# Memory attention, tanh-shrink and maxout on one core: token tiles of 320, 512, 320 over two batches, undivided runs of small matmuls, conversions begun earlier, one softmax for both parities

## The chip, the cores and the metric

The kernel runs on one core of a Trainium2 chip. The time is the device time of one execution in microseconds (us); the figure for a kernel is the median of its runs. One execution was recorded by the hardware profiler, and all profile rows are from it. Engines: PE multiplies matrices (PEld is its weight load), DVE, ACT and POOL work elementwise, SP issues most DMAs.

## The reference

Eight batches of 576 tokens, 8 heads of 64, 32 memory slots per head:

```python
a   = softmax(phi, axis=seq)                       # [8, 8, 576, 32]
k_m = einsum('bhsm,bhsd->bhmd', a, k); v_m = einsum('bhsm,bhsd->bhmd', a, v)
x   = softmax(q @ k_m^T / 8) @ v_m                 # -> [4608, 512]
h   = x @ w_in                                     # [512, 2048]
x   = (h - tanh(h)) @ w_out                        # [2048, 512]
m   = max(x @ w1, x @ w2, x @ w3)                  # three of [512, 768]
out = m @ w_out2                                   # [768, 512]
```

The weight matrices arrive as 64-bit floats, the rest as 32-bit floats.

## The kernel before

**Arithmetic.** A large product is made of three matmuls (`mm3`): each operand is split into a rounded part and a rest, and high x high, high x rest and rest x high are added in PSUM. `conv` turns a 64-bit weight block into such a pair: one DMA, an absolute value on ACT, five DVE instructions (lines 107, 108, 110, 112, 113), then POOL and ACT. One block of 128 x 512 (or 128 x 384) is called a conversion here.

**Stages.** The attention weights are never multiplied with `v_m` alone: `vw_gen` multiplies each head's `v_m` with its rows of `w_in` (the tile `vw`, by 8 small matmuls of 64 x 32 weights), and h = attention weights x `vw`, with a contraction of 256. The 2048 hidden features are worked in two phases of 1024. In phase 0 the attention of each batch is made (`kv_gen`, then `q_gen`: scores `sc` by 8 small matmuls, a softmax for parity e = 0 and one for e = 1, the result in `at`, also stored to DRAM), and partial results x go to DRAM; in phase 1 `at` is loaded again and the partial results are added. The last stage (lines 583 to 623) does the three-way maximum and the output.

**Steps.** A step is one tile of 288 tokens times one slice of 128 hidden features. Its work is 6 matmuls `ps_h` (`emit_h`), the chain tanh on ACT, subtraction on DVE, rounding on ACT, rest on POOL (`emit_g`, lines 399 to 403, the tile `gh`), and 12 matmuls `ps_x` (`emit_x`). Phase 0 and phase 1 have 128 steps each. In phase 0 the first two batches go twice over the tokens, four slices each time. `ps_x` has four PSUM banks, `ps_h` two, and the small matmuls share two banks under one tag `m`.

**Order.** Two queues of generators are advanced between matmul groups by `slot`: `fg` for the attention of coming batches and `vw`, `bg` for conversions; each entry has a step before which it doesn't start (a gate), and `rate` says how many advances a slot makes (in quarters). `need` runs an entry to its end. A list scheduler then places the emitted instructions, so that the order on an engine isn't that of the code. Conversions of the last stage's weights (`wb_conv`, `wz_conv`, stored to DRAM as `wb_d`, `wz_d`) and of `w_out`'s second half enter `bg` after the attention's pool is closed, at step 116.

Of the kernel before, what the change touches and what calls it, by code (L numbers as in the profile page):

```python
# [7 lines left out]
F32 = mybir.dt.float32  # L8
# [14 lines left out]
def kernel(  # L23
# [28 lines left out]
    C = 5  # L52
# [8 lines left out]
    LG = 2  # L61
    FC = 8
# [12 lines left out]
    ones = const.tile([P, P], F32, name="ones")  # L75
# [8 lines left out]
    ap = pool("attn", stack=attn)  # L84
    ps_x = pool("ps_x", PSUM, main)
# [42 lines left out]
    def wi_conv(fq):  # L128
        t = wi_p.tile([P, HP, FQ], F32, tag="wi", bufs=3, name="wi")
# [36 lines left out]
    def phi_gen(b):  # L166
# [6 lines left out]
        pm = ps_m.tile([P, 2, 2, P], F32, tag="m", bufs=2, name="ps_mx")  # L173
# [9 lines left out]
        V.tensor_tensor(out=ph, in0=ph, in1=pm[:, 1].rearrange("p i (h m) -> p (i h) m", m=M)[:, :, None, :].to_broadcast([P, H, C, M]), op=ALU.subtract)  # L183
# [10 lines left out]
    def kv_mm(b):  # L194
        ph = ph_t.pop(b)
        ps = ps_m.tile([P, 2, 256], F32, tag="m", bufs=2, name="ps_kv")
# [22 lines left out]
        pt = ps_m.tile([P, 2, P], F32, tag="m", bufs=2, name="ps_t")  # L219
# [15 lines left out]
    def q_gen(b, hfs):  # L235
# [7 lines left out]
        for hf in hfs:  # L243
            qT = []
            for g in range(2):
                t = ap.tile([P, 2, NH], F32, tag="qT", bufs=3, name="qT")
# [5 lines left out]
            scs = [ps_m.tile([P, NH], F32, tag="m", bufs=2, name="sc") for e in range(2)]  # L252
            for r in range(HP):
                for e in range(2):
                    pp = slice(64 * e, 64 * e + 64)
                    T.matmul(scs[e][32 * r:32 * r + 32], kT[b][pp, r], qT[r // 2][pp, r % 2], start=True, stop=True)
            yield
            o = slice(hf * NH, (hf + 1) * NH)
            for e in range(2):
                s = ap.tile([P, JH, M], F32, tag="s", bufs=2, name="s")  # L260
                V.transpose(out=s.rearrange("p j m -> p (j m)"), in_=scs[e])
                st = ap.tile([P, JH, 3], F32, tag="st", bufs=2, name="st")
                V.reduce_max(st[:, :, 0], s, axis=AX.X)
                V.tensor_tensor(out=s, in0=s, in1=st[:, :, 0:1].to_broadcast([P, JH, M]), op=ALU.subtract)
                yield
                S.activation(s, s, AF.Exp, scale=0.125)
                yield
                V.reduce_sum(st[:, :, 1], s, axis=AX.X)
                V.tensor_scalar(st[:, :, 2], st[:, :, 1], 1e-9, None, ALU.add)
                V.reciprocal(st[:, :, 2], st[:, :, 2])  # L270
                yield
                G.tensor_tensor(out=s, in0=s, in1=st[:, :, 2:3].to_broadcast([P, JH, M]), op=ALU.mult)
                yield
                aT = ap.tile([P, NH], F32, tag="aT", bufs=2, name="aT")
# [11 lines left out]
    def vw_gen(ph, b, fq):  # L286
        while 2 * ph + fq not in wi:
            bg.need("wi")
        t = at_p.tile([P, 2, 2, FQ], F32R, tag="vw", bufs=4, name="vw")
        pss = [ps_m.tile([P, FQ], F32, tag="m", bufs=2, name="ps_w") for e in range(2)]  # L290
        for r in range(HP):
            for e in range(2):
                pp = slice(64 * e, 64 * e + 64)
# [363 lines left out]
```

## Time and profile before

| | us |
|---|---|
| median of 3 runs (1485.02 to 1493.65) | 1491.73 |
| profiled execution, own time | 1483.24 |
| its span, first to last instruction | 1481.5 |
| PE busy | 1401.1 (95%) |
| DVE busy | 657.2 (44%) |
| POOL busy | 475.3 (32%) |
| ACT busy | 443.9 (30%) |

Busy times are averages over stages that differ. Steps 0 to 16 end at about 156 us, step 112 begins at 463, phase 1 (step 128) at 522, the last stage at 881. Matmul records overlap, so what a matmul costs is read from start to start, not from its duration. A weight tile read as 64-bit halves or plain 32-bit floats gives two matmul records for an instruction.

### The profile page before, as it was taken

What the parts mean: (1) busy time and instruction counts of PE and PEld (TensorE: products, weight loads), DVE (VectorE), ACT (ScalarE), POOL (GpSimd) and SP (SyncE); (2) the same over time, 40 slices, a digit from 0 to 9 for tenths busy, and PEclk for the clock granted to TensorE, in tenths of its full rate; (3) what the DMA queues carried; (4) which work ended last, traced back from release to release, by engine and by line L of the source; (5) the groups of instructions that cost most, each with busy time, mean ns of one, the idle gap of its engine ahead of it and who ended that gap; (6) DMA issues with size and microseconds to landing.
All of it is one profiled execution on the core that took longest, in us unless ns stands there. A gap on an engine that the chain in (4) does not pass through costs nothing.

```text
span 1481.5 us, 23564 instructions
## 1 busy us (share of the span) xinstructions
PE 1401.1 (95%) x9344; PEld 1167.8 (79%) x9344; DVE 657.2 (44%) x1225; ACT 443.9 (30%) x975; POOL 475.3 (32%) x508
## 2 busy tenths in 40 slices
PE   2587999999999999999999999999999999999998
PEld 1264887988897778788899998888888888888887
DVE  3789945546557988677433231211212111111110
ACT  1244443445344444444433331111111111111110
POOL 0356434334436756465533322111111111111110
PEclk9986999999999999999999999999999999999999
DMA  7765736445514358876422135110101010100001
GB/s 182 169 197 156 211 116 161 113 117 141 144 55 165 108 178 252 278 215 206 159 97 65 62 129 206 36 36 29 44 15 43 17 48 15 45 20 15 15 15 43
DMA packets 199150, 159.87 MB, mean 108 GB/s; under 512 B 96128, under 2 KB 182144, under 8 KB 197248
## 3 DMA queue, kind: packets, MB, share of 16 engines
q1 hardware_dynamic: 197312, 145.79, 34.0%
q0 software_dynamic: 1728, 12.58, 2.4%
q8 instruction: 73, 1.20, 0.3%
q14 instruction: 37, 0.30, 0.1%
HBM read 105.64 MB, written 52.69 MB: 107 GB/s over the span
## 4 chain that ended last, share of the span: by engine, by line
PE 77%; DVE 10%; DMA 5%; SPq 4%; issue 2%; ACT 2%; POOL 1%; DVEq 0%; POOLq 0%; ACTq 0%
PE ps_w L95 10%; PE ps_w L94 10%; PE ps_w L93 10%; PE ps_x L93 7%; PE ps_x L94 7%; PE ps_x L95 7%; PE ps_h L93 4%; PE ps_h L94 3%; PE ps_h L95 3%; PE ps_o L94 3%; PE ps_o L93 3%; PE ps_o L95 3%; PE ps_w L294 3%; SPq L161 2%; DVE cvb L110 2%
## 5 line engine op out<-in xcount | busy, mean ns | idle before, releaser
L403 POOL TENSOR_TENSOR gh<-th,gh 128x288 fp32r<-128x288 f32 x256 | 217.2, 851 | 312.6 <-ACT gh L402 257.3
L94 PE MATMUL ps_x<-gh,wo 128*128 128x288 f32 x1024 | 300.5, 302 | 1.9 <-POOL gh L403 1.9
L95 PE MATMUL ps_x<-gh,wo 128*128 128x288 f32 x1024 | 294.8, 297 | 0.0
L93 PE MATMUL ps_x<-gh,wo 128*128 128x288 f32 x1024 | 264.2, 303 | 1.8 <-DVE xo L443 1.0
L95 PE MATMUL ps_w<-xh,wb 128*128 128x512 f32 x648 | 254.9, 393 | 0.0
L94 PE MATMUL ps_w<-xh,wb 128*128 128x512 f32 x648 | 254.4, 393 | 0.0
L93 PE MATMUL ps_w<-xh,wb 128*128 128x512 f32 x648 | 253.8, 392 | 0.0
L597 POOL TENSOR_TENSOR mh<-m,mh 128x512 fp32r<-128x512 f32 x54 | 71.1, 1318 | 489.0 <-ACT mh L596 489.0
L94 PEld LDWEIGHTS ps_x<-gh,wo 128*128 128x128 f32 x1024 | 195.2, 191 | 26.5 <-issue 16.0
L93 PEld LDWEIGHTS ps_x<-gh,wo 128*128 128x128 f32 x1024 | 180.1, 192 | 24.7 <-issue 14.2
L400 DVE TENSOR_TENSOR th<-ps_h,th 128x288 f32<-128x288 f32 x256 | 114.4, 449 | 184.8 <-ACT th L399 184.4
L95 PEld LDWEIGHTS ps_x<-gh,wo 128*128 128x128 f32 x1024 | 194.8, 191 | 0.7 <-issue 0.5
L93 PE MATMUL ps_h<-at,vw 128*128 128x288 f32 x512 | 160.0, 313 | 27.6 <-DVE th L400 15.8
L593 DVE TENSOR_TENSOR m<-ps_w,m 128x512 f32<-128x512 f32 x54 | 37.3, 692 | 305.6 <-PE ps_w L95 305.6
L399 ACT ACTIVATE th<-ps_h 128x288 f32<-128x288 f32 x256 | 105.0, 410 | 177.7 <-PE ps_h L95 169.1
L402 ACT CAST gh<-th 128x288 fp32r<-128x288 f32 x256 | 110.0, 432 | 157.2 <-DVE th L400 145.7
L94 PE MATMUL ps_h<-at,vw 128*128 128x288 f32 x512 | 155.5, 304 | 1.6 <-POOL at L278 1.5
L95 PE MATMUL ps_h<-at,vw 128*128 128x288 f32 x512 | 154.7, 303 | 0.0
L93 PEld LDWEIGHTS ps_h<-at,vw 128*128 128x128 f32 x512 | 98.4, 193 | 57.7 <-DVE th L400 24.4
L94 PEld LDWEIGHTS ps_w<-xh,wb 128*128 128x128 f32 x648 | 121.7, 188 | 27.9
L93 PEld LDWEIGHTS ps_w<-xh,wb 128*128 128x128 f32 x648 | 121.7, 188 | 27.5
L95 PEld LDWEIGHTS ps_w<-xh,wb 128*128 128x128 f32 x648 | 121.7, 188 | 27.2
(81 smaller groups left out, 1783.6 us busy)
## 6 DMA issues: line engine op xcount, KB each, us to landing
xd<-xo SPq DMA_DIRECT2D x36, 576.0 KB, 3.8
raw<-in_moe_w_out_dram SPq DMA_DIRECT2D x22, 512.0 KB, 4.3
qt<-in_q_dram SPq DMA_DIRECT2D x128, 72.0 KB, 3.1
at_d<-at SPq DMA_DIRECT2D x16, 576.0 KB, 3.8
at<-at_d SPq DMA_DIRECT2D x8, 1152.0 KB, 5.9
raw<-in_moe_w_dram SPq DMA_DIRECT2D x24, 384.0 KB, 3.6
wb_d<-cs SPq DMA_DIRECT2D x72, 128.0 KB, 3.4
xo<-xd SPq DMA_DIRECT2D x16, 576.0 KB, 4.2
```

The lines of the kernel that those rows point to most:

```text
L93: T.matmul(o, w[0], x[0], start=start, stop=False)
L94: T.matmul(o, w[0], x[1], start=False, stop=False)
L95: T.matmul(o, w[1], x[0], start=False, stop=stop)
L110: V.scalar_tensor_tensor(out=b, in0=hw, scalar=0xC0000000, in1=b, op0=ALU.bitwise_and, op1=ALU.bitwise_or)
L161: DMA.dma_start(out=t[64 * e + 32 * h:64 * e + 32 * h + 32, r], in_=src[e, h, r])
L294: T.matmul(pss[e][32 * r:32 * r + 32], vT[b][pp, r], wi[2 * ph + fq][pp, r], start=True, stop=True)
L399: S.activation(th, ps, AF.Tanh)
L400: V.tensor_sub(th, ps, th)
L402: S.copy(gh[:, 0], th)
L403: G.tensor_sub(gh[:, 1], th, f(gh[:, 0]))
L593: V.tensor_max(m, pss[1], m)
L597: G.tensor_sub(mh[:, 1], m, f(mh[:, 0]))
```

## The change

**Tiles.** The two batches that phase 0 begins with keep tiles of 288. All other tokens go in pairs of batches: 1152 tokens as tiles of 320, 512 and 320. The tile of 512 holds 256 tokens of either batch, so its `ps_h` is made of two groups of 6 matmuls with 256 columns each. Phase 0 has 104 steps, phase 1 96. Partial results lie in one DRAM tensor `xd[0]`; the second pass over the first two batches loads and adds the first, so that phase 1 adds one block and no second one (`xb` goes).

**Small matmuls.** The two banks get tags of their own, `m0` and `m1`. `small` makes the first of a group's 8 matmuls also wait until DVE has released bank 1, and ties the 8 in their order.

**Softmax.** Both parities lie in one tile of 18 x 32, so one maximum, subtraction, exponential, sum and so on does what two did; the two transposes out of PSUM stay.

**Conversions.** The last stage's weights enter `bg` at step 32 instead of step 116. `wi_conv(2)` moves from a gate at step 36 to the point where the attention's pool is closed (step 90), ahead of `w_out`'s second half. Gates and rates change: `kv_gen` still 20 steps before a batch's first step, `q_gen` 16, `vw` 8 and 6, each also held until a buffer is free; rates fall from 10 and 8 to 6 and 2 at step 32, `bg` back to 8 at step 90.

**Last stage.** The input x is loaded in four pieces through two buffers instead of in one.

```diff
+    def bank(i, shape, name):
+        return ps_m.tile(shape, F32, tag=f"m{i}", bufs=1, name=name)
+    def small(mms):
+        ins = [T.matmul(o, w, x, start=True, stop=True).ins for o, w, x in mms]
+        if freed[1] is not None:
+            tc.add_manual_dep(ins[0], freed[1].name, ...Sync..., reason="both banks")
+        for a, b in zip(ins, ins[1:]):
+            tc.add_manual_dep(b, a.name, ...NoSync..., reason="side by side")
...
-            scs = [ps_m.tile([P, NH], F32, tag="m", bufs=2, name="sc") for e in range(2)]
+            scs = [bank(e, [P, NH], "sc") for e in range(2)]
+            small([(scs[e][32 * r:32 * r + 32], kT[b][...], qT[r // 2][...]) for r in range(HP) for e in range(2)])
...
-            for e in range(2):
-                s = ap.tile([P, JH, M], F32, tag="s", bufs=2, name="s")
+            s = ap.tile([P, J2, M], F32, tag="s", bufs=1, name="s")
+            for e in range(2):
+                freed[e] = V.transpose(out=s[:, e * JH:(e + 1) * JH]..., in_=scs[e]).ins
...
-            V.tensor_sub(t[:, e, 1], pss[e], f(t[:, e, 0]))
+            freed[e] = V.tensor_sub(t[:, e, 1], pss[e], f(t[:, e, 0])).ins
...
+                tiles[ph] += [pieces(t0, 320), pieces(t0 + 320, 512), pieces(t0 + 832, 320)]
...
+        for b, s0, n in pcs:
...
+            for kc in range(2):
+                mm3(ps[:, c0:c0 + n], (w[:, kc, 0, f0:f0 + P], w[:, kc, 1, f0:f0 + P]), (at[:, 0, kc, o], at[:, 1, kc, o]), kc == 0, kc == 1)
...
+        add = ph or t0 < NXI and fc >= 4
+        if fc == 4 and add or final and not add:
+            emit_x.xo = ga_p.tile([P, KD, NT], F32, tag="xo", bufs=1, name="xo")[:, :, :nt]
+            if add:
+                DMA.dma_start(out=emit_x.xo, in_=xd[0][:, :, o])
...
-    bg.add("wi", wi_conv(2), 36)
...
+            aq = max([s0 - AHEAD + 4] + [last_u[bb - 3, fq] - LG for fq in range(2) if bb > 2])
...
+    for g in last_w:
+        bg.add("last", g, start[0, 2])
+    rate[:] = 6, 2
...
+    bg.add("wi2", wi_conv(2))
     bg.add("wo1", chain(*[wo_conv(fc, wo1) for fc in range(8, 16)]))
```

On PE, in phase 0, this is the place of one `vw` group of batch 3 (`vT_92`; line 294 before) among the `ps_x` matmuls of one step.

```order
L93 MATMUL ps_x_2492<-gh,wo_1107 128x288
L294 MATMUL ps_w<-wi,vT_92 32x512 x2
L94 MATMUL ps_x_2490<-gh,wo_1107 128x288
L95 MATMUL ps_x_2490<-gh,wo_1107 128x288
L94 MATMUL ps_x_2491<-gh,wo_1107 128x288
L95 MATMUL ps_x_2491<-gh,wo_1107 128x288
L94 MATMUL ps_x_2492<-gh,wo_1107 128x288
L95 MATMUL ps_x_2492<-gh,wo_1107 128x288
L294 MATMUL ps_w<-wi,vT_92 32x512 x6
L93 MATMUL ps_x_2493<-gh,wo_1107 128x288
```

The same group in the changed kernel (the small matmuls are line 106 now):

```order
L94 MATMUL ps_x_2134<-gh,wo_944 128x320
L94 MATMUL ps_x_2135<-gh,wo_944 128x320
L106 MATMUL ps_w<-wi,vT_92 32x512 x8
L95 MATMUL ps_x_2132<-gh,wo_944 128x320
L96 MATMUL ps_x_2132<-gh,wo_944 128x320
```

The 8 matmuls stood in two pieces around six others and now stand together. Over the whole order `vw` stands in 74 such runs before and 45 now, for 32 groups, and the scores `sc` in 20 and 16, for 16 groups.

On DVE, at the start of the stretch with most conversions (step 113 before), `cva` and `cvb` are the conversions' tiles and `th` is the subtraction that PE's next steps need:

```order
L113 SCALAR_TENSOR_TENSOR cva<-raw,cva 128x512
L443 COPY xo<-ps_x_5151 128x288
L400 TENSOR_TENSOR th<-ps_h,th 128x288
L443 COPY xo<-ps_x_5153 128x288
L107 TENSOR_SCALAR cva<-cva 128x512
L108 TENSOR_SCALAR cvb<-cva 128x512
L110 SCALAR_TENSOR_TENSOR cvb<-raw,cvb 128x512
L107 TENSOR_SCALAR cva<-cva 128x512
L112 TENSOR_SCALAR cva<-cvb 128x512
L400 TENSOR_TENSOR th<-ps_h,th 128x288
```

In the changed kernel, at steps 88 to 90, the corresponding stretch reads:

```order
L434 TENSOR_TENSOR th<-ps_h,th 128x512 x2
L122 TENSOR_SCALAR cva<-cva 128x512
L123 TENSOR_SCALAR cvb<-cva 128x512
L125 SCALAR_TENSOR_TENSOR cvb<-raw,cvb 128x512
L122 TENSOR_SCALAR cva<-cva 128x512
L127 TENSOR_SCALAR cva<-cvb 128x512
L123 TENSOR_SCALAR cvb<-cva 128x512
L128 SCALAR_TENSOR_TENSOR cva<-raw,cva 128x512
L125 SCALAR_TENSOR_TENSOR cvb<-raw,cvb 128x512
L127 TENSOR_SCALAR cva<-cvb 128x512
L128 SCALAR_TENSOR_TENSOR cva<-raw,cva 128x512
L434 TENSOR_TENSOR th<-ps_h,th 128x512
```

Up to ten conversion instructions, two whole conversions, stand between two subtractions where five stood.

On SP, in the second pass over the first two batches, the store of one tile's sums (`xd`) and the load of the next tile's partial sums (`xo`) now stand like this; before, this pass had no load:

```order
L472 DMA xd_109<-xo 512x1x288
L333 DMA wb_d_97<-cs 128x2x128
L333 DMA wb_d_98<-cs 128x2x128
L333 DMA wb_d_99<-cs 128x2x128
L115 DMA raw<-in_moe_w_dram 128x768
L295 DMA at_d_1399<-at 512x1x288
L458 DMA xo<-xd_109 128x4x288
```

The load stands behind stores of a conversion's result and of an attention result, which wait for POOL.

## Rows read from the trace of the kernel before

**Rows 1.** The page: granted TensorE clock in 40 slices of 37 us, tenths of full speed.
```profile
PEclk9986999999999999999999999999999999999999
```

**Rows 2.** Stages: us, busy (count) by engine, granted clock, DMA share, GB/s.
```profile
0.00:156.20 156.20, 95.91 (x749) 63.19 (x750) 115.94 (x208) 46.07 (x97) 63.23 (x67) 0.87 0.68 174
156.20:209.40 53.20, 51.99 (x524) 43.47 (x523) 40.34 (x85) 23.96 (x58) 24.09 (x28) 1.00 0.69 195
209.40:264.00 54.60, 52.23 (x525) 44.86 (x524) 28.08 (x62) 21.13 (x52) 18.99 (x25) 0.97 0.48 120
264.00:313.00 49.00, 49.00 (x527) 43.33 (x526) 28.15 (x63) 21.34 (x52) 19.01 (x25) 1.00 0.53 134
463.00:522.00 59.00, 53.52 (x355) 42.61 (x354) 53.82 (x77) 27.06 (x61) 41.14 (x35) 1.00 0.38 132
522.00:623.00 101.00, 94.88 (x637) 78.43 (x637) 78.73 (x146) 45.31 (x108) 59.76 (x65) 0.97 0.74 235
840.50:859.50 19.00, 19.00 (x146) 19.00 (x145) 5.12 (x12) 6.65 (x16) 6.48 (x8) 1.00 0.20 63
880.80:1481.50 600.70, 595.83 (x2593) 486.56 (x2592) 107.74 (x161) 91.47 (x156) 75.27 (x62) 1.00 0.14 45
```

**Rows 3.** The tanh of line 399 in one stage: us, ACT busy (count).
```profile
840.50:859.50 19.00, 3.29 (x8) 1.00 0.20 63
```

**Rows 4.** Small matmuls of line 294 by stage: PE busy, PEld busy.
```profile
463.00:522.00 59.00, 9.47 (x46) 1.30 (x46) 1.00 0.38 132
522.00:623.00 101.00, 14.60 (x80) 1.97 (x80) 0.97 0.74 235
```

**Rows 5.** PE in order of time, last stage: start, us, what.
```profile
1000.01 0.39 PE L93 MATMUL ps_w<-xh,wb 128*128 128x512 f32 x1
...
1009.99 0.39 PE L95 MATMUL ps_w<-xh,wb 128*128 128x512 f32 x1
```

**Rows 6.** PE in order of time around a part and a whole small group.
```profile
345.47 1.06 PE L294 MATMUL ps_w<-wi,vT 64*32 64x512 f32 x8
...
784.05 0.29 PE L95 MATMUL ps_h<-at,vw 128*128 128x288 f32 x1
784.27 1.09 PE L294 MATMUL ps_w<-wi,vT 64*32 64x512 f32 x16
785.29 0.40 PE L93 MATMUL ps_h<-at,vw 128*128 128x288 f32 x1
785.53 0.29 PE L94 MATMUL ps_h<-at,vw 128*128 128x288 f32 x1
```

**Rows 7.** DVE groups by shape: busy us, mean ns, idle before.
```profile
L400 DVE TENSOR_TENSOR th<-ps_h,th 128x288 f32<-128x288 f32 x256 | 114.4, 449 | 184.8 <-ACT th L399 184.4
L299 DVE TENSOR_TENSOR vw<-ps_w,vw 128x512 fp32r<-128x512 f32 x64 | 42.4, 681 | 19.4 <-ACT vw L297 19.1
L110 DVE SCALAR_TENSOR_TENSOR cvb<-raw,cvb 128x512 uint32<-128x512 uint32 x38 | 33.7, 887 | 0.7
L113 DVE SCALAR_TENSOR_TENSOR cva<-raw,cva 128x512 f32<-128x512 uint32 x38 | 33.6, 884 | 0.7
L108 DVE TENSOR_SCALAR cvb<-cva 128x512 uint32<-128x512 uint32 x38 | 28.2, 741 | 0.7
L107 DVE TENSOR_SCALAR cva<-cva 128x512 f32<-128x512 f32 x38 | 24.9, 656 | 18.0 <-ACT cva L105 17.8
L112 DVE TENSOR_SCALAR cva<-cvb 128x512 uint32<-128x512 uint32 x38 | 23.7, 624 | 0.4
L110 DVE SCALAR_TENSOR_TENSOR cvb<-raw,cvb 128x384 uint32<-128x384 uint32 x24 | 18.1, 754 | 0.5
```

**Rows 8.** One line alone: DVE line 110, ns min/median/max.
```profile
L110 DVE SCALAR_TENSOR_TENSOR cvb<-raw,cvb x62: 541/692/1761, 30.7 to 717.8; 128x512 uint32<-128x512 uint32 x38, 128x384 uint32<-128x384 uint32 x24
```

**Rows 9.** What PE waited for after 16 us: us, times, longest.
```profile
PE ps_h L93 <- DVE th L400: 15.8, 12, 2.8
```

**Rows 10.** DMA issues: count, KB each, median us to landing.
```profile
xd<-xo SPq DMA_DIRECT2D x36, 576.0 KB, 3.8
xo<-xd SPq DMA_DIRECT2D x16, 576.0 KB, 4.2
```

More of the change, by code (lines that the diff above doesn't have):

```diff
@@ L84 @@
     ap = pool("attn", stack=attn)
+    ones = ap.tile([P, P], F32, name="ones")
     ps_x = pool("ps_x", PSUM, main)
@@ L265, in q_gen @@
[L265 to L274, printed above, removed]
@@ L287, in vw_gen @@
         while 2 * ph + fq not in wi:
-            bg.need("wi")
+            bg.need("wi2")
         t = at_p.tile([P, 2, 2, FQ], F32R, tag="vw", bufs=4, name="vw")
[L290 to L293, printed above, removed]
-                T.matmul(pss[e][32 * r:32 * r + 32], vT[b][pp, r], wi[2 * ph + fq][pp, r], start=True, stop=True)
+        pss = [bank(e, [P, FQ], "ps_w") for e in range(2)]
+        small([(pss[e][32 * r:32 * r + 32], vT[b][64 * e:64 * e + 64, r], wi[2 * ph + fq][64 * e:64 * e + 64, r])
+               for r in range(HP) for e in range(2)])
         yield
@@ L362, in slot, with pieces @@
                 tr.step(now[0])
[L365 to L374 removed]
+    def pieces(t0, n):
+        out, t = [], t0
+        while t < t0 + n:
+            b, s0 = divmod(t, NS)
+            k = min(t0 + n - t, NS - s0)
+            out.append((b, s0, k))
+            t += k
+        return t0, n, out
@@ L411, in emit_x @@
     def emit_x(i):
-        ph, b, s0, fc, first, final = steps[i]
+        ph, (t0, nt, pcs), fc, first, final = steps[i]
         while 8 * ph + fc not in wo_t:
@@ L447, in emit_x @@
         if final:
-            DMA.dma_start(out=d[:, :, s0:s0 + NH], in_=xo)
+            DMA.dma_start(out=xd[ph][:, :, o], in_=emit_x.xo)
     hooks = {}
@@ L486 @@
     bg.add("wo", chain(*[wo_conv(fc, wo_p) for fc in range(1, 4)]))
-    bg.add("wo", chain(*[wo_conv(fc, wo_p) for fc in range(4, FC)]), 10)
-    bg.add("wi", wi_conv(2), 36)
+    bg.add("wo", chain(*[wo_conv(fc, wo_p) for fc in range(4, FC)]), 6)
+    last_w = [wb_conv(w, kc, g) for g in range(2) for w in range(3) for kc in range(KD)] + [wz_conv(j) for j in range(J)]
     fg.add("kv", kv_gen(1))
@@ L517 @@
     wo1 = wo1_p.__enter__()
+    bg.q, rest = bg.q[:1], bg.q[1:]
+    bg.add("wi2", wi_conv(2))
     bg.add("wo1", chain(*[wo_conv(fc, wo1) for fc in range(8, 16)]))
-    for g in range(2):
-        for w in range(3):
-            for kc in range(KD):
-                bg.add("wb", wb_conv(w, kc, g))
-    for j in range(J):
-        bg.add("wb", wz_conv(j))
-    run(start[0, B - 1] + 4, start[1, 0] - 2)
+    bg.q += rest
+    rate[1] = 8
+    run(start[0, B - 1] + 2, start[1, 0] - 2)
     bg.need("wo1")
+    rate[1] = 2
     run(start[1, 0] - 2, start[1, 0])
```

188 lines of the change are left out of this document (99 added, 89 removed).

## The prediction

> **What bounds the kernel now.** I read the stages first [rows 2], then the order of PE inside them, then who waits. In the last stage PE is busy 595.8 of 600.7 us; its matmuls are neither fewer nor smaller after the change, so I carry it over at 600.7. Before it, three pictures alternate. From 840.5 to 859.5 nothing but steps runs: 8 tanh [rows 3] in 19.0 us, so a step of 18 matmuls of 288 columns costs 2.375 us, one matmul 132 ns. From 264 to 313 one batch's attention is added: 49.0 us for 16 steps, 38.0 of them steps and 11.0 attention on PE, with DVE busy only 28.2 us. From 463 to 623 the conversions are added: 160 us for 48 steps; DVE is busy 53.8 of 59.0 us (91%) in the first part, and PE waits for DVE's subtraction, 15.8 us in 12 places of the whole trace [rows 9]. The first 156 us are DVE's too: 115.9 us busy, PE 95.9, and the granted clock is 0.87 there, with slices at 0.8 and 0.6 [rows 1, 2], which is the 1.2 GHz level for part of them. So PE sets the end nearly everywhere after 156 us, and DVE where conversions crowd.
>
> **Runs of small matmuls.** A whole group takes 784.27 to 785.29; from the matmul ahead of it (784.05) to the second behind it (785.53) are 1.48 us instead of two gaps of 132 ns, so a run costs 1.21 us [rows 6]. A part of a group costs nearly the same: 1.06 us against 1.09 for sixteen records [rows 6]. The price is thus per run and not per matmul. By the order there are 74 runs of `vw` before and 45 after, of which 7 and 4 fall into the first 16 steps, where DVE decides; from 67 to 41 are 26 x 1.21 = 31.5 us. Two runs of `sc` fewer after step 16, priced somewhat lower since they stream 288 columns: 2. A run that must wait for both banks is placed later in the order; I price the wait at nothing, because the order puts a step's `ps_x` matmuls ahead of it. Without that cover the step's other matmuls, queued behind it on PE, and the tanh that waits for them are late: rival 3.
>
> **Matmul counts.** 512 columns take (1009.99 - 1000.01) / 44 = 226.8 ns, first and last of 45 starts [rows 5]. With 132 ns for 288 the line has 0.423 ns a column and 10.1 ns a matmul: 145.5 ns for 320, 118.4 for 256. A slice of a pair of batches needs 3 x 12 `ps_x` matmuls where four tiles of 288 need 48: 12 fewer, 96 in eight slices, 672 over the 7 pairs of both phases (3 and 4); `ps_h` keeps its count, 6 + 12 + 6 for 4 x 6. That gives 672 x 10.1 = 6.8 us. No row has 256 columns with full weights: if such a matmul took the 132 ns of 288, 672 of them would take back 9.1 us; if it took half of 226.8, 3.3 more would be gained. I take the line, as both neighbours lie on it.
>
> The Trainium skill (TensorE: Matmul & The Clock Gate, Back-to-back issue gap) gives a lone matmul N / 2.4 + 2.5 ns at full clock. By that the 672 would be worth 672 x 2.5 = 1.7 us, an estimate from the page, instead of 6.8; the trace's 226.8 ns for 512 columns lies 11 ns above that formula, and the sum goes by the rows.
>
> **Stalls that go.** 463 to 623 holds 160 us; 48 steps are 114.0, the small matmuls 9.47 + 14.60 = 24.1 us busy [rows 4], that is 22 runs at 1.09, or 26.6 us by the full price. 19.4 us are left: waits for DVE, small gaps, and a clock of 0.97. By the new order 17 of the 24 conversions of 384 columns stand before step 56, so this stretch changes its shape: I take these 19.4 out and put in the new ones below. 209 to 264 took 54.6 against 49.0 [rows 2]; with one run more there, 4 of the 5.6 are a stall of the old order, and I let them go too.
>
> **The first 156 us.** DVE bounds them. Merged softmaxes save the fixed part of six instructions on each half of a batch: four halves, some 1 us each, 4 us. The bounds are 0 (nothing, if the chain of waits and not the load decides) and 10 (the slices at the lower clock shrink too).
>
> **New load on DVE.** Here I add DVE's work between tanh subtractions, in its new order, and compare it with PE's steps. A conversion of 512 columns is 887 + 884 + 741 + 656 + 624 ns = 3.79 us [rows 7]; one of 384, scaled by 754 / 887, 3.2. A batch's attention with its `vw` and copies is 28.15 - 16 x 0.449 = 21.0 us [rows 2, 7].
> - Steps 88 to 104: 14 conversions (53.1), one of 384 begun (1.9), 8 `vw` subtractions at 0.681 (5.4), the tanh subtractions (8 at 0.48, 8 at 0.68: 9.3), half a batch's softmax and four copies (7): 77 us. PE there: 8 steps of 512 (12 x 226.8 + 12 x 118.4 ns = 4.14 us), 8 of 320 (2.62), 7 runs: 62.6 us. At the 91% that DVE reached in its fullest stretch, 77 would take 85, 22 too long; a lead of about two steps absorbs some 5. I take 18, from bounds of 5 (all of the lead, and DVE fully busy) and 33 (conversions a sixth dearer).
> - Steps 16 to 56: 17 conversions of 384 and 2 of 512 (62), three batches' attention (63), tanh subtractions (20), 16 additions of the second pass (7): 152 us, against PE with 113 us of steps and 3 x (11.0 - 1.2) of attention, 142. Same bound, 167; but the second pass leaves PE three or more steps ahead by the order. 11, from 0 to 36. This holds the second pass's reload as well: store 3.8, load 4.2 [rows 10] and two issues make more than 8 us against the 9.5 us of four steps, so its cover is thin, and SP has stores waiting for POOL in between.
> - Steps 64 and 88: the odd batch of a pair is needed 8 steps after the even one; the order shows PE's lead falling from three steps to two there. Two waits of 2 us, under the longest of 2.8 [rows 9]: 4, from 0 to 6.
> - Phase 1 until step 128, with 11 conversions left: 3, from 0 to 8.
>
> The conversions' stores `wb_d` move along. Where they stood the DMA share was 0.74, where they go it is 0.69 and 0.48 [rows 2]; I price that at nothing, and its loss of cover is in the 36 above.
>
> Phase 1 beyond that has DVE idle before and after, and dropping `xb`'s additions there gains nothing.
>
> **Sum.** -31.5 - 2 - 6.8 - 19.4 - 4 - 4 + 18 + 11 + 4 + 3 = -31.7 us. On the profiled execution's own 1483.2 that is 1451.5; on the median, which is 8.5 higher, 1460. I forecast the middle, 1456.
>
> **Rivals.**
> 1. DVE's backlog vanishes in PE's lead. For: 264 to 313 shows DVE far from full beside attention. Against: 91% in 463 to 522 already cost PE. Then 31 of the 36 us of new stalls fall away: 1425. Chance 0.20.
> 2. Slower: DVE becomes the bound of steps 16 to 56 and 88 to 104. The place is the subtraction `th` standing behind two conversions; the point is reached when a conversion beside attention and longer POOL instructions costs 4.5 us instead of 3.79. Line 110 alone ranges from 541 to 1761 ns [rows 8]. Then 162 and 87 us of DVE work at 91% are 178 and 96 against 142 and 62.6 of PE: 69 instead of 29, and with the waits at 64 and 88 no longer covered some 4 more: 1500. For: those ranges; against: the mean held over stages that were as full. Chance 0.07.
> 3. The runs become whole, but PE stands waiting for both banks. If half of the 41 runs wait the 1.3 us that a wait for DVE takes on the mean [rows 9], 27 us come back: 1483. For: the second phase still has 23 runs in parts, which shows banks being late; against: 8 of 8 together is where the order put them while other work was at hand. Chance 0.12.
>
> The Trainium skill (SBUF — State Buffer, Who interferes with whom) says that a DVE instruction in a two-port mode or with two SBUF inputs and a POOL instruction exclude each other for a whole instruction. By that, POOL instructions of 512 columns instead of 288 hold a conversion up longer, which speaks for rival 2; the spread of line 110 (541 to 1761 ns, an extra of up to 1.2 us) agrees with such blocking.
>
> **Numbers.** My own case, 1456 with 1436 to 1476, has 0.61. Less than 0.5% (about 7.5 us, what a measurement of this kernel tells from no change) counts as the same. Faster: all but 0.01 of my case, rival 1, half of rival 3, 0.86; same: the other half of it, 0.02 of rival 2 and the 0.01, 0.09; slower: the rest of rival 2, 0.05. The range takes in rival 1's price and stops short of rival 2: 1425 to 1482.
>
> **What would show it.** The last stage must again take about 601 us. Runs in the trace of phase 0 must have 16 records each, and small matmuls' busy time must fall by some 30 us. Stage times: about 152 us to step 16, 150 to 155 for steps 16 to 56, 78 to 82 for steps 88 to 104, 81 for a pair in the later phase 1 (75 of steps, five runs). DVE must be busiest (over 90%) in steps 88 to 104 and PE's waits for `th` must lie there. I am wrong if the gain comes with the old number of runs, if PE waits at the small matmuls for DVE, or if the second phase, which has DVE to spare, gains less than 25 us.

## The result and the profile after

The changed kernel took 1503.71 us (median of 7 runs, 1497.64 to 1506.05) against 1485.22 us for the kernel before on the same chip (7 runs): over all runs a ratio of 1.010, with a 95% interval of 1.0073 to 1.0128. The forecast was 1456 us, range 1425 to 1482: wrong in sign and outside the range. The profiled execution has a span of 1498.0 us and an own time of 1499.8 us, 16.5 us more than before by either.

The stages of the changed kernel, in the columns of [rows 2]: steps 0 to 16, 16 to 56, 56 to 88, 88 to 104 (the end of phase 0), 104 to 128, the rest of phase 1, the last stage:
```profile
0.00:158.20 158.20, 87.14 (x747) 62.96 (x747) 113.81 (x185) 45.48 (x91) 64.29 (x61) 0.86 0.65 171
158.20:334.80 176.60, 155.07 (x1480) 128.51 (x1479) 139.44 (x246) 72.73 (x154) 93.29 (x90) 0.96 0.78 216
334.80:472.50 137.70, 131.76 (x1370) 111.63 (x1368) 75.61 (x131) 53.58 (x109) 50.33 (x47) 1.00 0.42 115
472.50:551.50 79.00, 64.14 (x342) 48.63 (x343) 75.04 (x96) 31.84 (x61) 50.38 (x39) 0.96 0.42 137
551.50:649.80 98.30, 88.08 (x536) 72.55 (x535) 61.74 (x98) 40.91 (x85) 54.10 (x49) 0.95 0.65 215
649.80:897.30 247.50, 247.50 (x1613) 220.25 (x1614) 70.40 (x130) 82.39 (x165) 75.12 (x75) 1.00 0.23 78
897.30:1498.00 600.70, 595.88 (x2594) 486.67 (x2592) 109.08 (x161) 92.83 (x158) 74.01 (x62) 1.00 0.15 46
```
The last stage is the same to 0.1 us, so the 16.5 us lie ahead of it. To see what they are, the stretch from step 16 to the last stage in one row, first before, then after:
```profile
156.20:880.80 724.60, 709.37 (x6007) 618.11 (x6006) 433.55 (x858) 306.38 (x723) 336.78 (x380) 0.99 0.48 146
```
```profile
158.20:897.30 739.10, 686.55 (x5336) 581.57 (x5335) 422.24 (x698) 281.44 (x569) 323.23 (x298) 0.98 0.47 142
```
Length less PE's busy time is PE's idle time: 15.2 us before, 52.5 after. **PE works 22.8 us less and waits 37.3 us longer.** With 2.0 us more up to step 16 that is the 16.5. The saving of work came about, and more than all of it was given back in waits. The longest waits of PE after step 16 (what waited <- what released it: us, times, longest), first in the kernel before, then in the changed one:
```profile
PE ps_h L93 <- DVE th L400: 10.2, 10, 1.9
PE ps_w L294 <- DVE s L261: 2.0, 1, 2.0
PE ps_x L94 <- POOL gh L403: 1.9, 7, 0.6
```
```profile
PE ps_h L94 <- DVE th L434: 15.6, 17, 1.9
PE ps_x L94 <- ACT gh L436: 6.6, 1, 6.6
PE ps_w L106 <- DVE vw L312: 6.5, 5, 2.3
PE ps_x L95 <- POOL gh L437: 6.1, 12, 1.2
PE ps_w L106 <- POOL wi L131: 4.8, 1, 4.8
PE ps_mx L190 <- DVE vw L312: 4.5, 4, 1.7
```
The wait for the tanh subtraction grew from 10.2 to 15.6 us ([rows 9] has 15.8, but counts the first 156 us too). New are waits of small matmuls for the subtraction `vw`, which frees their bank (11.0 us in two lines; `ps_mx` are transposes that use bank 1 too), one wait of 4.8 us for a converted block of `w_in` (`wi`), and longer waits for `gh`. One of the waits for `vw` in full, on PE and then on DVE (start, us, what, in brackets idle before and releaser):
```profile
537.37 0.31 PE L94 MATMUL ps_h<-at,vw 128*128 128x320 f32 x1
...
539.22 0.31 PE L94 MATMUL ps_x<-gh,wo 128*128 128x320 f32 x1
...
539.95 0.31 PE L96 MATMUL ps_x<-gh,wo 128*128 128x320 f32 x1
542.61 1.04 PE L106 MATMUL ps_w<-wi,vT 64*32 64x512 f32 x2 [2.35 <-DVE vw L312]
543.58 0.42 PE L94 MATMUL ps_h<-at,vw 128*128 128x320 f32 x1
```
```profile
535.84 0.48 DVE L434 TENSOR_TENSOR th<-ps_h,th 128x320 f32<-128x320 f32 x1
536.24 1.34 DVE L122 TENSOR_SCALAR cva<-cva 128x512 f32<-128x512 f32 x1
537.61 0.98 DVE L123 TENSOR_SCALAR cvb<-cva 128x512 uint32<-128x512 uint32 x1
538.63 1.67 DVE L125 SCALAR_TENSOR_TENSOR cvb<-raw,cvb 128x512 uint32<-128x512 uint32 x1
540.33 0.43 DVE L127 TENSOR_SCALAR cva<-cvb 128x512 uint32<-128x512 uint32 x1
540.67 0.68 DVE L312 TENSOR_TENSOR vw<-ps_w,vw 128x512 fp32r<-128x512 f32 x1
541.27 0.68 DVE L128 SCALAR_TENSOR_TENSOR cva<-raw,cva 128x512 f32<-128x512 uint32 x1
541.88 0.68 DVE L312 TENSOR_TENSOR vw<-ps_w,vw 128x512 fp32r<-128x512 f32 x1
542.48 0.48 DVE L434 TENSOR_TENSOR th<-ps_h,th 128x320 f32<-128x320 f32 x1
```
The first small matmul starts when both `vw` subtractions are done; these stand behind four conversion instructions that take 4.4 us. Behind it on PE stand six `ps_h` matmuls that need neither subtraction. But they need a bank: of the two that `ps_h` has, the one freed by the subtraction at 535.84 went to the matmuls from 537.37 on, and the other is freed by the subtraction at 542.48, which stands behind the same conversion instructions and ends at 542.96. Without the small matmul ahead of them they could have started some 0.6 us earlier, no more. So two parts of the change meet here, the wait for both banks and the conversions; in this place the conversions set most of the time, and the experiments take the two apart.

### The profile page after: what moved, and what is told of

Its sections match the earlier page's. It is cut to its first block, busy times and chain, and to the rows that moved or that the text cites. A ratio compares the mean times of both kernels' runs of the same rounds, so it can differ in the third digit from the quotient of the medians.

```text
span 1498.0 us, 21579 instructions
## 1 busy us (share of the span) xinstructions
PE 1369.6 (91%) x8672; PEld 1131.2 (76%) x8672; DVE 645.1 (43%) x1043; ACT 419.8 (28%) x817; POOL 461.5 (31%) x420
## 4 chain that ended last, share of the span: by engine, by line
PE 66%; DVE 13%; DMA 8%; SPq 5%; issue 3%; POOL 3%; ACT 2%; DVEq 0%; ACTq 0%; POOLq 0%
PE ps_w L96 10%; PE ps_w L95 10%; PE ps_w L94 10%; PE ps_x L94 5%; PE ps_x L95 5%; PE ps_x L96 5%; DMA wb_d<-cs 3%; PE ps_o L95 3%; PE ps_o L94 3%; PE ps_o L96 3%; PE ps_h L94 3%; PE ps_h L96 3%; PE ps_h L95 3%; DVE cvb L125 2%; SPq L176 2%
## 5 line engine op out<-in xcount | busy, mean ns | idle before, releaser
L437 POOL TENSOR_TENSOR gh<-th,gh 128x320 fp32r<-128x320 f32 (+2 forms) x200 | 209.7, 1050 | 320.3 <-ACT gh L436 311.4
L95 PE MATMUL ps_x<-gh,wo 128*128 128x320 f32 (+2 forms) x800 | 271.0, 341 | 6.7 <-POOL gh L437 6.5
L94 PE MATMUL ps_x<-gh,wo 128*128 128x320 f32 (+2 forms) x800 | 257.0, 343 | 11.8 <-ACT gh L436 6.6
L96 PE MATMUL ps_x<-gh,wo 128*128 128x320 f32 (+2 forms) x800 | 265.6, 335 | 0.7 <-POOL wo L137 0.7
L434 DVE TENSOR_TENSOR th<-ps_h,th 128x320 f32<-128x320 f32 (+2 forms) x200 | 106.4, 534 | 197.8 <-ACT th L433 197.7
L94 PE MATMUL ps_h<-at,vw 128*128 128x320 f32 (+2 forms) x512 | 160.1, 313 | 32.5 <-DVE th L434 20.9
L94 PEld LDWEIGHTS ps_x<-gh,wo 128*128 128x128 f32 x800 | 150.8, 194 | 38.9 <-issue 17.7
L95 PEld LDWEIGHTS ps_x<-gh,wo 128*128 128x128 f32 x800 | 154.5, 193 | 27.9 <-POOL gh L437 14.5
L96 PEld LDWEIGHTS ps_x<-gh,wo 128*128 128x128 f32 x800 | 153.8, 193 | 10.9 <-issue 1.0
L625 DVE TENSOR_TENSOR m<-ps_w,m 128x512 f32<-128x512 f32 x54 | 37.3, 691 | 283.0 <-PE ps_w L96 283.0
L96 PE MATMUL ps_h<-at,vw 128*128 128x320 f32 (+2 forms) x512 | 155.5, 305 | 1.0 <-DVE vw L312 1.0
L95 PE MATMUL ps_h<-at,vw 128*128 128x320 f32 (+2 forms) x512 | 155.1, 303 | 0.0
L436 ACT CAST gh<-th 128x320 fp32r<-128x320 f32 (+2 forms) x200 | 99.7, 499 | 162.4 <-DVE th L434 150.6
L433 ACT ACTIVATE th<-ps_h 128x320 f32<-128x320 f32 (+2 forms) x200 | 94.8, 476 | 177.1 <-PE ps_h L96 168.8
```

What stands on the lines that cost most here:

```text
L433: S.activation(th, ps, AF.Tanh)
L434: V.tensor_sub(th, ps, th)
L436: S.copy(gh[:, 0], th)
L437: G.tensor_sub(gh[:, 1], th, f(gh[:, 0]))
L625: V.tensor_max(m, pss[1], m)
```

## The experiments

Theory A: the conversions beside the attention. Theory B: the fixed banks and the wait for both. Theory C: the tiles across two batches. Ratios are to the kernel before, run beside each kernel on the same chip (its median was 1483.9 to 1485.3 us in the five sets), taken over all runs, with their 95% intervals; they can differ by 0.001 from the ratio of two medians. The edits are shortened; `...` marks what is left out.

**1. Conversions after the attention again** (changed kernel, `e1_late`)
```
-    for g in last_w: bg.add("last", g, start[0, 2])
-    rate[:] = 6, 2
+    rate[:] = 6, 8
 ...
     bg.add("wo1", ...)
+    for g in last_w: bg.add("last", g)
```


> The changed kernel with one part undone: the conversions of the last stage's weights start only when the attention is finished (after step 90 of phase 0, eight pieces of work per four slots, as in the kernel before), everything else stays. Theory A (the conversions beside the attention hold up ACT, DVE and SyncE's queue, and PE waits for these): steps 16 to 104 shrink from 393 us to 355 to 370, the stretch after step 104 gives back some 5 to 15 us, time 1465 to 1485 us. Theory B (the two shared banks and the both-banks wait of the small matmuls do it): steps 16 to 104 stay at 385 to 395 us, time 1497 to 1510 us. Theory C (tiles across two batches need the odd batch 8 steps after the even one): as B.

1483.72 us, ratio 0.9989 (0.9971 to 1.0007). Theory A: the time is at the upper end of what was expected, and steps 16 to 104 took 372.5 us, just over the 370. Steps 16 to 56 of this kernel:
```profile
153.10:310.90 157.80, 146.17 (x1473) 124.91 (x1472) 86.19 (x157) 56.77 (x120) 55.67 (x56) 0.99 0.58 153
```
18.8 us less than 176.6, DVE 53 us less busy. Steps 104 to 200 took 11 us more (356.7 against 345.8), which is what the conversions cost where they stand now. The first 16 steps, ahead of the edit, were 5.1 us shorter (153.1 for 158.2); why is open.

**2. A deeper buffer for the conversions** (changed kernel, `e2_cab3`)
```
-        t = cv_p.tile([P, 2, 512], F32R, tag="cs", bufs=1, name="cs")
+        ab = cv_p.tile([P, 2, 512], U32, tag="cvab", bufs=3, name="cvab")   # in place of cva, cvb, cs
```


> The changed kernel, with the conversions where the change puts them, but without the single buffer cs: the two halves of a converted weight are written in place into a pair of work tiles that has three buffers, and stored from there. Theory A1 (ACT's rounding waits for the store that still reads cs, and tanh waits behind it): steps 16 to 104 shrink from 393 us by 15 to 30 us, and the 8.7 us wait of ACT's rounding at 559 us goes; time 1470 to 1488 us. Theory A2 (it is the number of instructions and the place of the stores in SyncE's queue, not the buffer): time within 6 us of the changed kernel's 1504 us. B and C: no change, 1497 to 1510 us.

1503.17 us, 1.0130 (1.0098 to 1.0161): A2. One place had seemed to matter most: ACT waits for the single buffer `cs`, tanh stands behind it, and PE waits 6.6 us for `gh` (the second line of the waits above):
```profile
569.35 0.51 ACT L135 CAST cs<-cva 128x384 fp32r<-128x384 f32 x1 [8.69 <-DMA wb_d<-cs]
569.76 0.43 ACT L433 ACTIVATE th<-ps_h 128x320 f32<-128x320 f32 x1
```
It was the largest single wait, and its stretch did shrink (steps 104 to 128: 91.6 us for 98.3), but the time did not: the largest wait of a trace need not be what sets the time.

**3. Tiles of 288** (changed kernel, `e3_t288`)
```
-  tiles[ph] += [pieces(t0, 320), pieces(t0 + 320, 512), pieces(t0 + 832, 320)]
+  tiles[ph] += [pieces(t0 + i * NH, NH) for i in range(4)]
```


> The changed kernel with tiles of 288 tokens of one batch throughout (four in place of 320, 512, 320), all else as changed. Theory C (the pairs of batches make the attention late): steps of 16 to 56 us lose their waits, time 1475 to 1490 us. Theories A and B: the waits stay, the number of matmuls and of tanh, subtraction and rounding instructions goes up again; a pair of batches takes 0.5 to 2 us longer in either phase, time 1500 to 1520 us.

1486.66 us, 1.0014 (0.9997 to 1.0030): by its time theory C, but not by its reason, since steps 16 to 56 did not get shorter (179.7 us for the same tokens); the gain is scattered. Experiment 11 turns its sign.

**4. No added dependences** (changed kernel, `e4_loose`)
```
-        if freed[1] is not None: tc.add_manual_dep(ins[0], freed[1].name, ..., reason="both banks")
-        for a, b in zip(ins, ins[1:]): tc.add_manual_dep(b, a.name, ..., reason="side by side")
```


> The changed kernel without the two added dependences of the small matmuls (the first no longer waits for both banks, and the eight need not stand side by side); the banks themselves stay as changed. Theory B: the waits for the subtraction of vw go from in front of the big matmuls, time 1480 to 1495 us. Theories A and C: the runs that are split again cost 1.2 us each, waits elsewhere stay; time 1500 to 1515 us.

1485.92 us, 1.0014 (0.9996 to 1.0032): theory B. Steps 16 to 56 take 178.4 us (176.6 with the dependences); steps 88 to 104 fall from 79.0 to 69.3, though DVE also has 11.4 us less to do in them (63.7 for 75.0), since work moved to the steps behind. So A and B both hold, and mostly in different places.

**5. Only the small matmuls' part** (kernel before, `f3_b_small`)
```
-        pss = [ps_m.tile([P, FQ], F32, tag="m", bufs=2, name="ps_w") for e in range(2)]
-        for r in range(HP): ...
+        pss = [bank(e, [P, FQ], "ps_w") for e in range(2)]
+        small([...])                     # likewise sc, ps_mx, ps_kv, ps_t
```

> The kernel before with one part of the change alone: two banks of one tile each for the small matmuls, and each group of eight put side by side behind the release of both banks; tiles, softmaxes and conversions as before. The prediction's step (about 26 runs fewer at 1.2 us each, nothing lost): TensorE's busy time up to the last stage falls by some 25 to 30 us and the time to 1455 to 1467 us. Theory W (the busy time falls, but TensorE then waits as much longer, since the chain from the banks' release to the next group sets the pace): time 1480 to 1490 us. Theory B (the wait for both banks costs more than the runs did): 1492 to 1505 us.

1494.92 us, 1.0081 (1.0056 to 1.0106): theory B. This row answers to the first of the two long rows in the section on the result:
```profile
160.70:889.80 729.10, 691.91 (x6007) 615.14 (x6005) 434.77 (x850) 301.81 (x721) 337.28 (x379) 0.99 0.48 144
```
PE busy 17.5 us less, idle 37.2 instead of 15.2, and the first 16 steps 4.5 us longer. The part on which the forecast counted most made the kernel before slower by itself; experiment 13 shows how much of that comes with the fixed banks alone.

**6. Only the conversions' part** (kernel before, `f4_b_spread`)
```
+    run(0, 32)
+    for g in last_w: bg.add("last", g, 32)
+    rate[1] = 2
+    run(32, start[0, B - 1] + 4)
 ...
```

> The kernel before with another part alone: the last stage's weights are converted from step 32 of phase 0 on, beside the attention, two pieces of work per four slots, instead of after it; all else as before. Theory A (the conversions beside the attention hold up what TensorE waits for): steps 16 to 64 (156.6 us before) take 170 to 180 us, steps 104 to 160 (187.3 us before) give back 5 to 20 us, time 1487 to 1500 us. The prediction's step (stalls in steps 112 to 160 go, the attention hides the conversions): 1465 to 1478 us.

1489.17 us, 1.0031 (1.0013 to 1.0050): theory A. Steps 16 to 64, 156.8 us before [rows 2, its second to fourth row], and steps 104 to 200, 303.1 us before:
```profile
155.80:331.80 176.00, 162.32 (x1586) 136.97 (x1585) 149.39 (x305) 81.96 (x200) 106.17 (x118) 0.96 0.78 210
465.10:745.30 280.20, 270.73 (x1969) 237.43 (x1969) 162.97 (x303) 119.01 (x274) 138.09 (x142) 0.99 0.45 149
```
19.2 us lost early (10 more in steps 64 to 104, 133.3 for 123.2), 22.9 given back late.

**7. Both undone** (changed kernel, edits 1 and 4, `f1_late_loose`)

> The changed kernel with two parts undone at once: conversions after the attention, and no dependences added to the small matmuls. Alone the first gave 1483.7 us and the second 1485.9 us, 20 and 18 us under the changed kernel. If the two costs lie in different places (conversions in steps 16 to 56, both banks in steps 88 to 104) they add: 1465 to 1472 us. If they are one and the same slack (either edit relaxes the one chain): 1478 to 1487 us.

1469.34 us, 0.9906 (0.9883 to 0.9929): the two costs add, and what is left of the change is worth 15 us. Its waits after step 16, complete:
```profile
PE ps_h L94 <- DVE th L430: 10.6, 15, 2.0
PE ps_x L95 <- POOL gh L433: 4.1, 5, 1.5
PE ps_x L94 <- DVE xo L461: 2.8, 2, 2.2
PE ps_mx L186 <- DVE vw L308: 2.6, 2, 1.6
PE ps_w L106 <- DVE vw L308: 1.7, 3, 0.7
```

**8. Edits 1 and 3 together** (`f2_late_288`)

> The changed kernel with conversions after the attention and tiles of 288 tokens of one batch throughout. Alone 1483.7 and 1486.7 us. If the two costs add: 1464 to 1471 us; if they are one slack: 1478 to 1487 us. The clean part of phase 1 gives the tiles' own price: 0.6 us less per pair of batches with 288 than with 320, 512, 320 (81.9 against 82.5 us in the runs so far).

1481.70 us, 0.9991 (0.9975 to 1.0008): the second case. With late conversions 288 gains nothing to speak of (1483.72 with the longer tiles).

**9. The two dependences apart** (edit 1 and one half of edit 4; `h2_sync` keeps the wait, `h1_chain` the order)
```
-        for a, b in zip(ins, ins[1:]): tc.add_manual_dep(b, a.name, ..., reason="side by side")     # h2_sync
-        if freed[1] is not None: tc.add_manual_dep(ins[0], freed[1].name, ..., reason="both banks")  # h1_chain
```

> The changed kernel with conversions after the attention, and of the two added dependences only one: the first of eight small matmuls waits until both banks are free, but the eight need not stand side by side. With both dependences 1483.7 us, with neither 1469.3 us. If the wait for both banks is the price (rival 3 of the prediction): 1480 to 1487 us. If it is the fixed order of the eight: 1467 to 1473 us.

> The changed kernel with conversions after the attention, and of the two added dependences only the other one: the eight small matmuls stand side by side, but the first does not wait for both banks. With neither dependence 1469.3 us (63 runs from step 16 to the last stage, TensorE idle for 22.3 us there), with the wait alone 1484.5 us (61 runs, 42.5 us idle). If whole groups without the wait save runs at about 1 us each and TensorE's idle time stays near 22 us: 1460 to 1468 us. If the second matmul of a group, standing in TensorE's queue behind the first, then waits for its bank and holds up all that follows: idle 35 to 45 us, 1478 to 1487 us.

The wait alone: 1484.51 us, 0.9996 (0.9982 to 1.0009). The order alone: 1478.22 us, 0.9956 (0.9933 to 0.9978). From step 16 on, with neither, with the wait, with the order:
```profile
150.90:867.10 716.20, 693.95 (x5336) 584.91 (x5335) 422.00 (x708) 281.12 (x573) 324.28 (x302) 0.99 0.49 148
```
```profile
148.60:881.70 733.10, 690.59 (x5334) 585.00 (x5324) 421.92 (x710) 280.21 (x571) 328.94 (x302) 0.98 0.48 145
```
```profile
152.00:876.10 724.10, 701.68 (x5282) 585.14 (x5275) 425.69 (x704) 280.47 (x571) 327.77 (x303) 0.99 0.48 147
```
Idle 22.3, 42.5 and 22.4 us. With the wait for both banks come the whole 20 us of idle time; it buys 3.4 us of work. The first expectation's first case holds. The order costs no waiting, but the eight did not become whole: 76 runs of small matmuls (`vw` and `sc`) in place of 63, and 7.7 us more work. That is neither case of its expectation: the idle time of the first, the time of the second. Whole groups without the wait were not had this way.

Where the idle time lies with the wait alone (three of the lines; for neither dependence see experiment 7):
```profile
PE ps_h L94 <- DVE th L432: 16.0, 11, 5.1
PE ps_w L106 <- POOL wi L129: 4.8, 1, 4.8
PE ps_w L106 <- DVE s L273: 3.8, 2, 2.2
```
Directly ahead of small matmuls stand 11.1 us, against 4.3 with neither: 7 of the 20 us. Of these, 4.8 are one wait for a converted block of `w_in`, which the changed kernel and `e1_late` have too, and `e4_loose` and `f1_late_loose`, without the wait for both banks, don't. The other 13 us lie ahead of the large matmuls, and the longest of these waits, 5.1 us at 616, comes of ACT, where tanh stands behind a rounding that waits for a load of the last stage:
```profile
614.39 0.62 ACT L576 CAST xh<-xr 128x512 fp32r<-128x512 f32 x1 [8.16 <-DMA xr<-xd]
```
So the dependence also moved other work to worse places. How much of the 20 us is waiting for the banks themselves was not separated.

**10. Conversions thin in phase 1; two softmaxes** (both on `f1_late_loose`)
```
     bg.need("wo1")
+    rate[1] = 3                                                        # h3_slow
-            s = ap.tile([P, J2, M], F32, tag="s", bufs=1, name="s")    # h4_two_softmax
+            for e in range(2):
+                s = ap.tile([P, JH, M], F32, tag="s", bufs=2, name="s")
 ...                                                                    # as before the change
```

> The changed kernel without the added dependences, and with the conversions after the attention, spread thinly over phase 1 (three pieces of work per four slots in place of eight from step 104 on). Theory A (what counts is how much DVE, ACT and POOL work stands beside TensorE's in one stretch): steps 104 to 160, 210.5 us with the dense conversions, come near to 195 us, nothing is paid in steps 160 to 200 where DVE is busy for a third of the time; time 1455 to 1463 us. If the conversions cost the same wherever they stand: 1466 to 1473 us.

> The changed kernel with conversions after the attention and no added dependences, and besides with a softmax for each parity as before the change (two buffers). The prediction's prices for the merged softmax (fewer fixed costs on DVE and ACT, some 4 us of waits less): 1471 to 1478 us. If the halves' overlap is worth more than the fixed costs: 1460 to 1467 us. If it is hidden: 1467 to 1472 us.

1471.38 us, 0.9903 (0.9875 to 0.9932): no gain. After the attention the conversions cost the same however dense they are, against theory A's finer form. Two softmaxes: 1478.09 us, 0.9949 (0.9933 to 0.9966), so the merged one is worth some 9 us; the first case, at its upper edge.

**11. Tiles of 288 without the other costs** (edits 1, 3 and 4, `i1_late_loose_288`)

> The changed kernel with conversions after the attention, no added dependences, and tiles of 288 tokens of one batch throughout. With 320, 512, 320 it took 1469.3 us. If the tiles are worth what the clean pairs of phase 1 show (0.6 us per pair in favour of 288, eight pairs): 1463 to 1470 us. If the longer tiles are worth the 6.8 us of the prediction: 1474 to 1480 us.

1490.19 us, 1.0039 (1.0021 to 1.0056), 21 us slower than with the longer tiles: neither expectation. The row from step 16, and the small `vw` matmuls there with 320, 512, 320 and then with 288 (busy, mean ns, idle before):
```profile
151.30:887.60 736.30, 713.35 (x6008) 618.31 (x6006) 432.22 (x786) 298.42 (x693) 337.27 (x358) 0.99 0.48 144
```
```profile
L106 PE MATMUL ps_w<-wi,vT 64*32 64x512 f32 x448 | 54.8, 602 | 1.7 <-DVE vw L308 1.7
```
```profile
L106 PE MATMUL ps_w<-wi,vT 64*32 64x512 f32 x448 | 72.9, 609 | 3.6 <-DVE s L271 2.8 <-DVE vw L308 0.7
```
Idle is alike (22.9 and 22.3 us); PE works 19.4 us longer, and 18.1 of it are the same 448 records in 66 runs instead of 48. So the longer tiles leave fewer groups cut in parts, and they do it without the dependences. The price of a run is thus confirmed with idle time held still: 1.0 us of `vw` busy time for each. With 288 the kernel is also 5 us slower than the kernel before, though the merged softmax is worth 9 (experiment 10): something else in the change costs, and what was not found.

**12. What of a conversion costs** (changed kernel)
```
-        DMA.dma_start(out=raw..., in_=src...)          # i4_work_only, with the stores of cs
+        raw = wo_t[0]...                               # read in place
-        S.activation(...); V...; G...                  # i5_dma_only
+        put(wo_t[0])                                   # the stores alone, after the load
```

> The changed kernel, its last conversions reduced to their instructions on ACT, DVE and GpSimd: they read a weight tile that lies in SBUF already, and nothing is loaded or stored for them (24 stores of that same tile at step 156 stand in, so the output is not the reference's). If the engines' work is what the attention and TensorE wait for: steps 16 to 56 stay at 170 to 180 us, time 1495 to 1505 us. If it is the transfers and SyncE's queue: steps 16 to 56 at 155 to 162 us, time 1483 to 1490 us.

> The changed kernel, its last conversions reduced to their transfers: each weight is loaded and a tile of the same size is stored at the pace of before, without any work on ACT, DVE and GpSimd between (the output is not the reference's). If the engines' work is the price: steps 16 to 56 at 155 to 162 us; and since no conversion remains anywhere, phase 1 stays at 248 us after step 128: time 1470 to 1485 us. If the transfers and the queue are the price: steps 16 to 56 at 170 to 180 us, time 1495 to 1505 us.

1508.44 us, 1.0155 (1.0137 to 1.0174), 3 us above its first case, and 1476.60 us, 0.9943 (0.9924 to 0.9963). Steps 16 to 56, the instructions alone, then the transfers alone:
```profile
157.20:334.50 177.30, 155.78 (x1475) 130.41 (x1475) 139.02 (x246) 73.60 (x154) 94.27 (x90) 0.93 0.51 137
```
```profile
159.70:322.80 163.10, 149.84 (x1477) 128.33 (x1476) 88.66 (x165) 56.75 (x122) 54.11 (x55) 0.97 0.69 191
```
Against 157.8 with neither, the instructions alone cost all 19 us and the transfers alone 5; the two don't add. It is the engines' work.

**13. Fixed or shared banks** (kernel before with edit 5 less its dependences, `h5_b_banks`; `f1_late_loose` with shared banks, `i6_shared_banks`)
```
-        return ps_m.tile(shape, F32, tag=f"m{i}", bufs=1, name=name)
+        return ps_m.tile(shape, F32, tag="m", bufs=2, name=name)        # i6_shared_banks
```

> The kernel before with the two single banks for the small matmuls and the changed order in which they are taken, but no added dependences. With the dependences 1494.9 us. If the dependences are the whole price: 1480 to 1487 us. If the fixed banks are part of it: 1488 to 1496 us. If fewer runs come of the banks alone and are worth their 1.2 us: below 1478 us.

> The changed kernel with conversions after the attention, no added dependences, and the small matmuls' two banks taken in turn from one pair as in the kernel before, in place of one fixed bank per parity. In the kernel before the fixed banks alone cost 7 us (1491.3 against 1484 us). If they cost the same here: 1460 to 1465 us. If the changed order of the work needs no turn-taking: 1467 to 1472 us.

1491.31 us, 1.0049 (1.0031 to 1.0068), and 1468.60 us, 0.9888 (0.9868 to 0.9909), level with the 1469.34 of experiment 7. The first kernel from step 16:
```profile
153.40:889.60 736.20, 717.13 (x5998) 620.82 (x5997) 431.35 (x861) 307.00 (x724) 338.10 (x380) 0.99 0.48 144
```
Fixed banks cost 7 us in the kernel before (four runs more, 7.8 us more work) and nothing that can be measured in the changed one. Set beside experiment 5, the row also tells what the dependences do with short tiles: `vw` in 50 runs instead of 72, 25.2 us less work for 18.1 us more idle time. There they do make groups whole and gain 7.1 us after step 16, and the first 16 steps take 7.3 us longer (160.7 for 153.4).

## Why the prediction was wrong

**The step that failed: "I price the wait at nothing".** The count of runs and the price of a run were near. From step 16 the 448 records of `vw` took 72.4 us before in 67 runs:
```profile
L294 PE MATMUL ps_w<-wi,vT 64*32 64x512 f32 x448 | 72.4, 605 | 2.0 <-DVE s L261 2.0
```
and in 41 runs after, of which 18 are whole:
```profile
L106 PE MATMUL ps_w<-wi,vT 64*32 64x512 f32 x448 | 46.2, 629 | 11.5 <-DVE vw L312 6.5 <-POOL wi L131 4.8
```
That is 26.2 us for 26 runs, against 28.3 by 1.09 us of busy time each [rows 6]. But the wait that was put at nothing costs 15 us alone (experiment 9, 1484.5 against 1469.3 us), with 20 us of idle time, and the two dependences together 18 (experiment 4). In the last column, what stands directly ahead of a group went from 2.0 to 11.5 us, 4.8 of it for the block of `w_in`; some 32 of the 52.5 us of idle time lie ahead of `ps_h` and `ps_x`. The cover I named was the step's `ps_x` matmuls ahead of the group; the row at 542.61 shows them used up. PE waits at the small matmuls for DVE, which I had named as a sign of being wrong.

Nor did the wait bring the runs. With late conversions `vw` has 46 runs with both dependences and 48 with neither; with early ones 41 and 46. Most of the saving is the longer tiles' (66 runs with 288, 48 without, experiment 11). I had named one cause of the fewer runs and not asked whether another part of the change brings them at no price. The mechanism is rival 3's, but not its size or its sign: its 1483 us still lay under the kernel before.

**Conversions, steps 16 to 56: +11 priced, 18.8 measured** (experiment 1), inside its bounds of 0 to 36. The stretch took 176.6 us for 153 forecast. That it comes near rival 2's 178 is chance: DVE was busy 139.4 of it, 79% and not the 91% of the rival, and a conversion of 512 columns cost 3.93 us, not 4.5 (with 4.5 for it and the 384 columns in proportion, the rival's 162 would have been 164). Of the 18.8 us, 9.9 are idle time of PE (21.5 against 11.6) and 8.9 are longer busy time for the same steps (155.1 against 146.2). Of the 21.5 us, 16.9 end with a DVE instruction, as at 540 us; that they are waits in order behind conversions is read from such rows and was not tested by itself. The spread that I gave the rival, 541 to 1761 ns, has its low end from 384 columns; with 512 it begins at 644. Line 125 shows longer instructions: the mean of 128x512 is 991 ns after and 887 before [rows 7]. The Trainium skill (SBUF — State Buffer, Who interferes with whom) says that a DVE instruction with two SBUF inputs contends with a POOL instruction that reads SBUF. Whether POOL's longer instructions matter by that is open: line 128, of the same kind, has 873 after and 884 before, and with tiles of 288 the mean of line 125 falls to 952 in experiment 3 and rises from 972 to 1023 in experiment 11.

**"Stalls that go", -19.4:** the same move gave back 22.9 us in the kernel before (experiment 6), but only 11 in the changed one (experiment 1). In the kernel before the attention took 29 us for it. The move doesn't pay in either kernel.

**Matmul counts, -6.8:** not borne out. The 320-column matmuls follow each other at 146 ns (539.22 to 539.95, five gaps), as priced, but the later phase 1, all work and no idle time, has 82.5 us for a pair of batches (247.5 for three) for the 81 forecast. With tiles of 288 (`e3_t288`) the three pairs took 245.6; less the small matmuls (16.05 us with 320, 512, 320 and 13.94 with 288) that leaves 231.5 and 231.7, so the lengths themselves are worth nothing. What the tiles are worth is elsewhere and larger: 21 us, nearly all through runs that are not cut (experiment 11), once the wait doesn't hide it. Why `e3_t288` is faster than the changed kernel is left open; it has both kinds of wait still in it.

**Merged softmax, -4 in the first 156 us:** wrong in place. These 156 us became 158.2; with the other costs gone two softmaxes have even the shorter start (146.2 us against 150.9), and the merged one gains 14.8 us after it. What sets the first 16 steps was not settled.

**Steps 88 to 104: 78 to 82 forecast, 79.0 measured,** DVE at 95%, but that is partly luck: 9.7 of it go when the dependences go (experiment 4). **Waits at steps 64 and 88, +4:** steps 56 to 88 had 6 us of idle time, the end of the range. **Stores `wb_d`, nothing:** nearly right; the one wait of 8.7 us at 569 cost 6.7 in its stretch and nothing in the total (experiment 2), and the transfers alone 5 in steps 16 to 56 (experiment 12). **Last stage:** right.

Of the 47.7 us between the 1456 forecast and the 1503.7 measured, the wait for both banks holds 15 to 18, and the conversions cost 17 to 20 where the sum had put a net of 12.6 (+18 +11 +3 -19.4); that is 20 to 25 us of it. Of the rest the stages show 6 in the first 16 steps (158.2 for 152) and 4.5 in the three later pairs of phase 1; some 15 us are not assigned to a step, since the parts act on each other and were not all undone one by one. By place, steps 56 to 88 and 104 to 128 took 236.0 us, where the forecast's other stage times leave some 221.

## What to carry to other kernels

A saving on the busiest engine counts only with the idle time beside it: read both from the same stretch, and price an added wait by what stands behind it on that engine, not by what stands ahead. Ask whether another part of the change already brings the saving that the wait is to bring: here the tiles did. Before work is moved under another stage, ask whether that stage's releases (here the subtraction that frees a bank) will queue behind it on an engine that works in order; 79% busy is enough to lose 19 us. Undo parts in pairs: alone, three different edits each brought the kernel to within 0.2% of the time before, and only undone together did two of them show a gain of 15 us.

## What was not expected of the hardware

A run of small matmuls costs about the same work whether it holds a whole group of 16 records or a part: 72.4, 54.8 and 46.2 us for 448 records in 67, 48 and 41 runs are 1.08, 1.14 and 1.13 us a run. The forecast priced it so; that it holds over whole kernels was not known.

The granted clock of steps 16 to 56 is 0.96 in the changed kernel and 0.99 with the conversions moved away. Of 176.6 and 157.8 us that is 7.1 and 1.6 us of clock lost, so by this estimate the clock holds at most 5.5 of the 8.9 us by which PE is busy longer. In the changed kernel PE stood at the lower level, 1.2 GHz, after the waits of that stretch, but not after every wait. Two windows, the first behind a wait of 1.85 us at 179.48, the second behind the one of 2.35 us at 542.61:
```profile
180.30:187.10 6.80, 5.65 (x33) 3.97 (x33) 6.00 (x13) 2.31 (x6) 4.10 (x5) 0.50 0.96 262
542.70:556.00 13.30, 11.77 (x68) 8.99 (x68) 13.03 (x17) 5.86 (x13) 10.33 (x10) 1.00 0.54 178
```
The length of one wait doesn't tell whether the clock falls.
